# A new list of steps for linear attention and a highway layer on one core, with two weight rows to a partition and more work on GpSimd and ScalarE

## The chip, the cores and the metric

The kernel runs on one core of one Trainium2 chip. The metric is the device time of one execution in microseconds (us); the median of three runs before the change is 120.71 us (120.66 to 121.03).

A core has a matrix engine (TensorE, PE in the profile; PEld is its loading of the stationary operand), a vector engine (VectorE, DVE), an activation engine (ScalarE, ACT), a general engine (GpSimd, POOL) and a queue engine that only issues transfers (SyncE, SP). Transfers between the chip's main memory and the on-chip memory SBUF run on 16 DMA engines. PE writes its results to a second on-chip memory, PSUM, which POOL cannot reach.

## What is computed

The reference, cut to its core:

```python
# q, k, v: (8, 8, 576, 64) float32
q_s = softmax(q, over the 64 features);  k_s = softmax(k, over the 576 rows)
kv = np.einsum('bhsd,bhse->bhde', k_s, v)
x = np.einsum('bhsd,bhde->bhse', q_s, kv)            # as (4608, 512)
H = np.maximum(x @ w_h, 0.0)
T = 1.0 / (1.0 + np.exp(-(x @ w_t + b_t)))
out = T * H + (1.0 - T) * x                           # (4608, 512) float32
```

The kernel writes the gate as T = (1 + tanh(z/2))/2, so that out = x + (tanh(z/2) + 1) * d, with d = max(x @ (w_h - I)/2, -x/2).

## The kernel before

The program has no loops over tiles at run time. A text constant, ORDER (lines 16 to 62), names some 700 steps, and the last lines of the kernel (483 to 487) call one small function for each of them in that order. Each engine then carries out its own instructions strictly in the order in which they were issued to it; semaphores make an instruction wait for what it reads and for the buffers it overwrites. A step is written kind_number(_part)(:engine). The same list orders the DMA queue of SP (loads k, q, v, w and most stores st) and that of ACT (b, and stores marked :A).

The work: eight batches b of 576 rows, 36 tiles i of 128 output rows each. Batches go in pairs: tiles 0 to 3 are batch 0's, 4 to 7 batch 1's, and tile 8 takes the last 64 rows of both; nine tiles for each pair.

- Loads: `k_b_c`, `v_b_c`, `q_b_j`, `w_h_c`, `w_t_c` (two pieces of 512 KB each for both weight matrices, line 210). The number after the batch is the piece. Three buffers each for q, k, v.
- `ek` (line 252) exponentiates k on ACT, `eq` (lines 297 to 305) q on ACT; `vc` (line 258) casts v to 16 bits on ACT, DVE or POOL.
- `kv` (line 268): 72 small products a batch on PE. `kr` and `kn` (lines 280, 286): DVE divides by the sums and writes the block matrix `kvb`.
- `qt` (lines 316, 321): PE turns exp(q); `qc` (line 330) copies it to SBUF on ACT or DVE.
- `xu` (line 350): PE multiplies a tile of exp(q) by `kvb`. `rs` and `x` (lines 359, 365): DVE divides, giving the tile x (16 bit, six buffers `x16`).
- `xt` (line 372): four PE transposes of x into the PSUM tile `turned`; `xe` (line 379) copies them to SBUF on ACT or DVE.
- `bw` (lines 387, 389): puts the bias into the gate's PSUM bank, by a copy on ACT (:A) or by a PE product (no mark). `mt` (line 399) adds the four products with w_t, `mh` (line 407) makes the four with w_h. Two banks each, `ps_t` and `ps_g`.
- `th` (lines 421, 423): tanh on ACT. `dd` (line 427): DVE makes d (three buffers).
- `uu` is the blend: on DVE straight from PSUM (line 437), or, for tiles marked :P anywhere in the list, on POOL in two steps, `g` = tanh + 1 (line 434) and `u` = g * d (line 435). For such tiles `th` writes SBUF instead of PSUM. Three buffers each for g, u and the tanh.
- `oo` (line 455): out = u + x, on POOL except the last half tile. `st` (lines 463, 471, 475): stores; most tiles are stored two together.
- `fill_n` (line 167): n dummy PE products on a zero tile into the unused half of `turned`. They change no result.
- `whd` (line 225) subtracts the identity from w_h's blocks, `whc` and `wtc` (lines 231, 218 to 221) cast the weights; `bp`, `bc`, `bsplit` prepare the bias.

Tiles 0, 4 and 5 are worked in two halves (the second number of the step), so that they can start with half the heads. The last tile, 35, is blended and stored in two halves of 256 columns.

Of the kernel before, what the change touches and what calls it, by code (L numbers as in the profile page):

```python
# [16 lines left out]
b_0 b_32 k_0_2 ek_0_3 q_0_0 setuppool setupdve k_0_0 eq_0_0 v_0_0 v_0_3 v_0_2 ek_0_2 bsplit ek_0_1 fill_16 vc_0_0:A  # L17
fill_16 fill_16 qt_0_0 vc_0_2 q_0_4 v_0_1 bp vc_0_3:D fill_16 bc w_h_2 kv_0_1 fill_12 eq_0_1 qc_0_0 w_h_0 w_t_0 vc_0_1
qt_0_1 whd_2:P w_t_2 q_1_0 kr_0_1 ek_0_0 kn_0_1 kv_0_0 fill_2 k_1_2 bw_3 kr_0_0 kn_0_0 whd_1:P whd_0:P fill_9 xu_0_0
whd_3 eq_0_2 xu_1_0 v_1_2 qc_0_1:A whc_2:A rs_0_0 rs_1_0 qt_0_2 x_1_0 x_0_0 qc_0_2:A fill_12 xt_1_0 whc_0:A v_1_0  # L20
xe_1_0:D k_1_0 bw_1 xu_3_0 q_1_4 wtc_0 xu_0_1 rs_3_0 x_3_0 mh_1_0 wtc_2 xt_3_0 xe_3_0 xu_2_0 mt_1_0 rs_0_1 x_0_1
xt_0_0 eq_1_0 q_2_0 mt_3_0 th_1_0 rs_2_0 xe_0_0:D vc_1_3 ek_1_3 x_2_0 xt_0_1 th_3_0 qt_1_0 xe_0_1:D ek_1_2 dd_1
vc_1_0:A mh_0_0 xt_2_0 k_2_0 xe_2_0:D vc_1_2:D uu_1_0:P mh_0_1 bw_2 dd_0 qc_1_0:A mh_2_0 dd_2 vc_1_1 v_2_0 kv_1_1
mh_3_0 ek_1_0 bw_0 kr_1_1 kn_1_1 dd_3 ek_1_1 mt_2_0 xu_5_1 rs_5_1 xu_4_1 kv_1_0 rs_4_1 k_3_0 x_5_1 th_2_0 kr_1_0 bw_5
oo_1_0 xt_5_1 mt_0_1 kn_1_0 mt_0_0 xu_5_0 x_4_1 rs_5_0 eq_1_1 xu_4_0 qt_1_1 xe_5_1 mt_5_1 x_5_0 eq_1_2 qc_1_1 xt_5_0
xe_5_0:D mh_5_1 th_0_0 q_3_0 rs_4_0 eq_2_2 uu_0_0 xu_6_0 rs_6_0 xt_4_1 qt_1_2 mt_5_0 mh_5_0 v_3_0 bw_4 x_4_0 x_6_0
xe_4_1 th_5_0 xt_4_0 mh_4_1 uu_3_0:P qc_1_2:A xe_4_0 xu_8_0 mh_4_0 mt_4_1 xt_6_0 mt_4_0 eq_2_0 dd_5 oo_0_0 uu_2_0:P
rs_8_0 oo_3_0 vc_2_2 uu_5_0 qt_2_0 x_8_0 ek_2_2 xe_6_0:D ek_2_0 k_4_0 dd_4 xu_7_0 rs_7_0 bw_6 th_4_0 oo_5_0 xt_8_0
mh_6_0 mt_6_0 q_4_9 x_7_0 xe_8_0:D xt_7_0 vc_2_0:A qc_2_0 eq_2_1 uu_4_0 oo_4_0 dd_6 bw_7:A kv_2_0 th_6_0 bw_8:A ek_3_0
ek_3_2 oo_2_0 xe_7_0:D mh_8_0 kr_2_0 kn_2_0 dd_8 mt_7_0 xu_9_0 rs_9_0 x_9_0 qt_2_1 th_7_0 mt_8_0 q_4_0 qc_2_1 uu_6_0:P  # L30
xu_10_0 oo_6_0 xt_9_0 rs_10_0 x_10_0 th_8_0 xe_9_0 mh_7_0 uu_8_0 qt_2_2 dd_7 bw_9 xu_12_0 eq_3_1 eq_3_0 xt_10_0 mt_9_0
mh_9_0 rs_12_0 x_12_0 xe_10_0:D uu_7_0:P xu_11_0 qc_2_2 xt_12_0 rs_11_0 qt_3_0 x_11_0 bw_10:A vc_3_2 dd_9 xe_12_0:D
vc_3_0:A th_9_0 uu_9_0 mh_10_0 oo_8_0 kv_3_0 kr_3_0 dd_10 xt_11_0 mt_10_0 eq_3_2 qc_3_0:A bw_12:A oo_7_0 kn_3_0
mh_12_0 xu_14_0 ek_4_2 mt_12_0 xe_11_0:D v_4_0 v_5_0 qt_3_1 ek_4_0 rs_14_0 x_14_0 dd_12 xt_14_0 xe_14_0:D k_5_0
xu_13_0 th_10_0 bw_11:A rs_13_0 mh_11_0 mt_11_0 x_13_0 th_12_0 q_5_0 xt_13_0 qc_3_1:A oo_9_0 dd_11 uu_10_0:P xu_15_0
qt_3_2 uu_12_0 rs_15_0 mh_14_0 eq_4_0 xe_13_0:D eq_4_1 mh_13_0 x_15_0 oo_10_0 xu_16_0 xt_15_0 qc_3_2 dd_14 rs_16_0
qt_4_0 th_11_0 bw_14:A k_6_0 mt_14_0 x_16_0 qc_4_0 vc_4_2:A xe_15_0:D st_1_1 xu_17_0 st_1_0 rs_17_0 oo_12_0 x_17_0
qt_4_1 dd_13 bw_13:A mt_13_0 th_14_0 fill_0 vc_4_0 kv_4_0 uu_11_0:P eq_4_2 xt_16_0 qc_4_1:A mh_15_0 v_6_0 qt_4_2
vc_5_2 q_5_9 uu_14_0 xe_16_0:D st_3_1 oo_11_0 kr_4_0 th_13_0 oo_14_0 kn_4_0 bw_16:A bw_15:A xt_17_0 ek_5_0 xe_17_0:D
dd_15 mh_16_0 xu_18_0 qc_4_2:A rs_18_0 mt_16_0 ek_5_2 x_18_0 vc_5_0 th_16_0 uu_13_0:P mt_15_0 dd_16 uu_16_0 xt_18_0  # L40
# [25 lines left out]
def kernel(  # L66
# [49 lines left out]
    spare = turned[:, 1].rearrange("p c d -> p (c d)").bitcast(FP32)  # L116
# [48 lines left out]
    def fill(e, n):  # L165
        for _ in range(n):
            nc.tensor.matmul(spare, blank[:, 0:P], blank[:, 0:2 * P], start=True, stop=True,  # L167
                             skip_group_check=True)
# [38 lines left out]
    def load_w(e, w, c):  # L207
        src = dict(t=moe_w_t, h=moe_w_h)[w]
        T[f"w{w}{c}"] = op.tile([P, 2, DM], FP32, tag="o32", name=f"w32{w}_{c}")
        nc.sync.dma_start(T[f"w{w}{c}"], src.rearrange("(c p) n -> p c n", p=P)[:, c:c + 2])  # L210
# [12 lines left out]
    def wh_less_identity(e, c):  # L223
        block = T[f"wh{c // 2 * 2}"][:, c % 2, c * P:(c + 1) * P]
        (nc.gpsimd if e == "P" else nc.vector).tensor_sub(block, block, idf)
# [23 lines left out]
    def ek(e, b, c):  # L249
        n = 1 if b < 2 else 2  # L250
        t = once(f"ek{b}", lambda: ekp.tile([P, NJ, 4, D], FP16, tag="ek", name=f"ek_{b}"))
        nc.scalar.activation(t[:, :, c:c + n].rearrange("p j c d -> p c j d"),  # L252
                             T[f"k32{b}"][:, c:c + n].rearrange("p c (j d) -> p c j d", j=NJ), AF.Exp)
# [39 lines left out]
    def eq(e, b, g):  # L293
        t = once(f"qe{b}", lambda: qep.tile([P, NJ, 4, D], FP16, tag="qe", name=f"qe_{b}"))
        j0, j1 = GROUPS[g]
        if b not in WIDE:
            nc.scalar.activation(t[:, j0:j1].rearrange("p j c d -> p c j d"),  # L297
                                 T[f"q32{b}"].rearrange("p c (j d) -> p c j d", j=NJ)[:, :, j0:j1], AF.Exp)
        elif g < 2:
            src = flat_q(b)[:, 0:MAIN].rearrange("p (c hh j d) -> p c hh j d", c=4, hh=2, j=4)  # L300
            dst = t.rearrange("p j c d -> p (j c d)")[:, 0:MAIN]
            dst = dst.rearrange("p (j hh c d) -> p c hh j d", j=4, hh=2, c=4)
            nc.scalar.activation(dst[:, :, g], src[:, :, g], AF.Exp)
        else:
            nc.scalar.activation(t[:, 8], flat_q(b)[:, MAIN:].rearrange("p (c d) -> p c d", c=4), AF.Exp)
# [212 lines left out]
```

## Time and profile before

| | |
|---|---|
| median of three runs | 120.71 us |
| the profiled execution, its own time | 120.66 us |
| its span on the profile | 118.8 us |
| PE busy | 112.4 us (95%) |
| ACT busy | 95.1 us (80%) |
| DVE busy | 94.3 us (79%) |
| POOL busy | 83.0 us (70%) |
| moved by DMA | 40.08 MB, mean 337 GB/s |

The profile page gives each engine's busy time and the busy share of each of 40 equal slices of the span as a digit (9 means 90% or more). A group row reads: line, engine, operation, output<-inputs, shape, count | busy time in us, mean duration in ns | idle time of that engine just before. The timeline lists start and duration in us. A chain of waits is followed back from the last instruction to what released it. Matmuls overlap in the array and their ends are modelled, so the distance from one start to the next is PE's true pace.

Six groups by shape, from the same execution:

| group | count | busy us | mean ns |
|---|---|---|---|
| bias product on PE, 512 columns (L389) | 9 | 3.4 | 378 |
| bias copy on ACT (L387) | 26 | 15.3 | 594 |
| exp of k, 128x1152 (L252) | 12 | 13.5 | 1161 |
| exp of k, 128x576 (L252) | 8 | 5.3 | 678 |
| blend on POOL, g (L434) and u (L435) | 17 each | 10.5 and 19.6 | 618 and 1155 |
| blend on DVE, 512 columns (L437) | 18 | 12.3 | 685 |

### The profile page before, as it was taken

How to read it: one execution, taken by the hardware profiler on the slowest of the kernel's cores; microseconds unless marked ns; L12 is line 12 of the kernel's file. 1: busy time of each engine (PE TensorE's matmuls, PEld its weight loads, DVE VectorE, ACT ScalarE, POOL GpSimd, SP SyncE). 2: the span in 40 equal slices, each digit the busy share in tenths (PEclk: the TensorE clock that was granted, in tenths of full speed). 3: DMA queues.
4: the chain of work that ended last, by engine and by line, in shares of the span. 5: the costliest groups of instructions: out<-in, count | busy, mean ns of one | idle time of the engine just before them, and what ended most of it. 6: DMA issues, size and time to landing. Idle time of an engine off the chain costs nothing.

```text
span 118.8 us, 3618 instructions
## 1 busy us (share of the span) xinstructions
PE 112.4 (95%) x1440; PEld 70.7 (59%) x1440; DVE 94.3 (79%) x225; ACT 95.1 (80%) x144; POOL 83.0 (70%) x93
## 2 busy tenths in 40 slices
PE   5997999999999999999999999999999999999970
PEld 3785786645656665665565666565665655554560
DVE  5604277697999978999989999879896999879880
ACT  4265679969698999999999999949979987578420
POOL 5002240199095999939999997996798939999960
PEclk9999999999999999999999999999999999999999
DMA  2999999999999999999999999999999942995564
GB/s 91 352 376 384 386 376 379 394 370 387 392 386 392 389 389 385 336 376 386 391 375 361 404 387 394 348 357 385 394 389 336 338 110 88 395 287 204 200 253 168
DMA packets 22596, 40.08 MB, mean 337 GB/s; under 512 B 3250, under 2 KB 9650, under 8 KB 22580
## 3 DMA queue, kind: packets, MB, share of 16 engines
q1 hardware_dynamic: 22352, 39.46, 92.7%
q10 hardware_dynamic: 228, 0.40, 1.3%
q8 instruction: 11, 0.18, 0.6%
q14 instruction: 5, 0.04, 0.1%
HBM read 30.41 MB, written 9.44 MB: 335 GB/s over the span
## 4 chain that ended last, share of the span: by engine, by line
PE 56%; DMA 26%; SPq 5%; ACT 5%; DVE 2%; issue 2%; DVEq 0%
PE gps L407 19%; PE tps L399 19%; DMA v<-in_v_dram 12%; DMA w32t<-in_moe_w_t_dram 7%; DMA k<-in_k_dram 6%; PE turned L372 6%; PE xu L350 5%; PE qps L316 3%; PE kv L268 3%; SPq L183 3%; SPq L205 2%; DVE u L437 1%; PE qps L321 1%; ACT tps L387 1%; ACT v L258 1%
## 5 line engine op out<-in xcount | busy, mean ns | idle before, releaser
L455 POOL TENSOR_TENSOR o<-u,x 128x512 f32<-128x512 f16 (+1 forms) x36 | 40.5, 1142 | 6.1 <-DVE u L437 5.6
L399 PE MATMUL tps<-w16t,xT 128*128 128x512 f16 (+1 forms) x148 | 37.1, 373 | 0.0
L407 PE MATMUL gps<-w16h,xT 128*128 128x512 f16 x144 | 36.9, 380 | 0.0
L365 DVE TENSOR_TENSOR x<-xu,rs 128x512 f16<-128x512 f32 (+1 forms) x39 | 25.0, 647 | 2.4
L427 DVE SCALAR_TENSOR_TENSOR d<-x,gps 128x512 f16<-128x512 f16 x36 | 24.3, 676 | 0.2
L258 POOL CAST v<-v 128x1152 f16<-128x1152 f32 (+1 forms) x11 | 10.7, 970 | 18.9 <-DMA v<-in_v_dram 17.6
L252 ACT ACTIVATE ek<-k 128x1152 f16<-128x1152 f32 (+1 forms) x20 | 18.9, 968 | 3.1 <-DMA k<-in_k_dram 3.1
L435 POOL TENSOR_TENSOR u<-g,d 128x512 f16<-128x512 f16 x17 | 19.6, 1155 | 1.4
L399 PEld LDWEIGHTS <-xT 128*128 128x128 f16 x148 | 13.4, 98 | 10.3
L407 PEld LDWEIGHTS <-xT 128*128 128x128 f16 x144 | 12.6, 98 | 11.6 <-ACT xT L379 0.6
L387 ACT COPY tps<-ball 128x512 f32<-128x512 f32 x26 | 15.3, 594 | 1.6 <-DVE u L437 1.2
L167 PE MATMUL turned<-blank 128*128 128x256 f16 x111 | 14.8, 292 | 1.3 <-POOL blank L149 1.3
L372 PE MATMUL turned<-idh,x 128*128 128x128 f16 x144 | 14.4, 219 | 0.2 <-ACT xT L379 0.2
L350 PE MATMUL xu<-kvb,eq 128*128 128x130 f16 (+1 forms) x160 | 14.3, 224 | 0.0
L350 PEld LDWEIGHTS <-eq 128*128 128x128 f16 (+1 forms) x160 | 10.3, 100 | 6.8 <-DVE x L365 2.3
L437 DVE SCALAR_TENSOR_TENSOR u<-tps,d 128x512 f16<-128x512 f32 (+1 forms) x20 | 13.1, 658 | 1.5 <-ACT tps L423 1.2
L423 ACT ACTIVATE tps<-tps 128x512 f32<-128x512 f32 (+1 forms) x20 | 11.2, 561 | 3.5 <-PE tps L399 3.3
L167 PEld LDWEIGHTS <-blank 128*128 128x128 f16 x111 | 11.3, 105 | 3.6 <-POOL blank L149 1.3
L372 PEld LDWEIGHTS <-x 128*128 128x128 f16 x144 | 10.3, 98 | 4.8 <-DVE x L365 0.6
L297 ACT ACTIVATE qe<-q 128x1024 f16<-128x1024 f32 (+1 forms) x12 | 10.0, 842 | 3.9 <-DMA q<-in_q_dram 3.8
L379 DVE COPY xT<-turned 128x512 f16<-128x512 f16 (+1 forms) x28 | 11.3, 403 | 2.2 <-PE turned L372 1.9
L434 POOL TENSOR_SCALAR g<-th 128x512 f16<-128x512 f16 x17 | 10.5, 618 | 3.6 <-ACT th L421 3.6
(48 smaller groups left out, 120.9 us busy)
## 6 DMA issues: line engine op xcount, KB each, us to landing
k<-in_k_dram SPq DMA_DIRECT2D x6, 1152.0 KB, 14.7
v<-in_v_dram SPq DMA_DIRECT2D x6, 1152.0 KB, 11.6
out_dram<-o SPq DMA_DIRECT2D x22, 256.0 KB, 4.9
q<-in_q_dram SPq DMA_DIRECT2D x10, 512.0 KB, 9.1
out_dram<-o SPq DMA_DIRECT2D x6, 512.0 KB, 5.5
k<-in_k_dram SPq DMA_DIRECT2D x4, 576.0 KB, 6.9
q<-in_q_dram SPq DMA_DIRECT2D x2, 1152.0 KB, 14.0
q<-in_q_dram SPq DMA_DIRECT2D x2, 640.0 KB, 12.3
```

The source lines that it names most:

```text
L167: nc.tensor.matmul(spare, blank[:, 0:P], blank[:, 0:2 * P], start=True, stop=True, skip_group_check=True)
L252: nc.scalar.activation(t[:, :, c:c + n].rearrange("p j c d -> p c j d"), T[f"k32{b}"][:, c:c + n].rearrange("p c (j d) -> p c j d", j=NJ), ...
L350: nc.tensor.matmul(dst, turned_q(b, jp, n), kvb[b % NKV][:, hh, kk], start=True, stop=True, skip_group_check=True)
L365: nc.vector.tensor_mul(t[:, k0:k1], sums(i, k)[:, :, :, 0:64], T[f"rs{i}_{k}"][:, 0:k1 - k0].unsqueeze(3).to_broadcast([P, k1 - k0, 4, D]))
L372: nc.tensor.matmul(t[:, n], T[f"x{i}"][:, n * P:(n + 1) * P], idh, is_transpose=True, start=True, stop=True, skip_group_check=True)
L387: nc.scalar.copy(t[:, cs], ball[:, cs])
L399: nc.tensor.matmul(T[gate(i, k)][:, cs], T[f"xT{i}"][:, n], w16["t"][:, n, cs], start=False, stop=(n == parts[-1] and not first), skip_gro ...
L407: nc.tensor.matmul(t, T[f"xT{i}"][:, n], w16["h"][:, n], start=(first and n == parts[0]), stop=(n == parts[-1] and not (first and len(part ...
L427: nc.vector.scalar_tensor_tensor(t, T[f"x{i}"], -0.5, T[f"gps{i}"], op0=ALU.mult, op1=ALU.max)
L435: nc.gpsimd.tensor_mul(t, g, T[f"d{i}"])
L437: nc.vector.scalar_tensor_tensor(t[:, cs], T[gate(i, h)][:, cs], 1.0, T[f"d{i}"][:, cs], op0=ALU.add, op1=ALU.mult)
L455: eng.tensor_add(t[:, cs], T[f"u{i}"][:, cs], T[f"x{i}"][:, cs])
```

## The change

1. Each load of weights puts rows 2p and 2p+1 of a 256-row half on partition p, one piece of 4096 bytes, instead of rows p and p+128 as two pieces of 2048. The contraction index is therefore paired differently, and the identity block and the transposes of x follow: they take every second column.
2. Dummies multiply 512 columns instead of 256 and write the whole of `turned`.
3. From batch 2 on, exps of q are cut by pieces of the row block instead of by columns, and steps marked :F do in one instruction what two or three did: eq_2, ek_2, ek_3, ek_5, eq_5, ek_6 and eq_7 (whole, or all but the last 256 columns).
4. 20 tiles are blended on POOL instead of 17, and 30 biases are copied by ACT instead of 26. All four identity subtractions and the cast of one half of w_t are on POOL.
5. For the last half tile the blend stays in PSUM and the addition reads it there; halves have their own `u16` tile.
6. The whole list of steps is new. 14 stores are on ACT's queue instead of 2.

```diff
 ORDER = """
-b_0 b_32 k_0_2 ek_0_3 q_0_0 setuppool setupdve k_0_0 eq_0_0 v_0_0 v_0_3 v_0_2 ek_0_2 bsplit ek_0_1 fill_16 vc_0_0:A
-fill_16 fill_16 qt_0_0 vc_0_2 q_0_4 v_0_1 bp vc_0_3:D fill_16 bc w_h_2 kv_0_1 fill_12 eq_0_1 qc_0_0 w_h_0 w_t_0 vc_0_1
-qt_0_1 whd_2:P w_t_2 q_1_0 kr_0_1 ek_0_0 kn_0_1 kv_0_0 fill_2 k_1_2 bw_3 kr_0_0 kn_0_0 whd_1:P whd_0:P fill_9 xu_0_0
-whd_3 eq_0_2 xu_1_0 v_1_2 qc_0_1:A whc_2:A rs_0_0 rs_1_0 qt_0_2 x_1_0 x_0_0 qc_0_2:A fill_12 xt_1_0 whc_0:A v_1_0
...
+setuppool fill_8 fill_8 v_0_0 q_0_0 eq_0_0 fill_8 fill_8 v_0_1 setupdve k_0_0 vc_0_0 fill_8 v_0_3 vc_0_3 k_0_2 v_0_2
+b_0 q_0_4 b_32 w_h_0 bsplit bp ek_0_0 vc_0_1 ek_0_1 kv_0_0 ek_0_2 qt_0_0 ek_0_3 w_h_2 vc_0_2 kv_0_1 kr_0_1 whd_1:P
+qc_0_0:A w_t_2 whd_0:P kr_0_0 fill_6 bc kn_0_1 xu_0_1 kn_0_0 xu_1_0 xu_0_0 bw_1 w_t_0 eq_0_1 qt_0_1 rs_1_0 x_1_0
+whd_2:P whc_0:A k_1_2 xt_1_0 rs_0_1 whd_3:P qc_0_1 xe_1_0 whc_2:A v_1_2 bw_3 xu_3_0 rs_3_0 fill_6 rs_0_0 eq_0_2 x_3_0
+xt_3_0 xe_3_0 xu_2_0 x_0_1 wtc_2 ek_1_2 mh_1_0 qt_0_2 xt_0_1 x_0_0 qc_0_2:A xt_0_0 q_1_0 xe_0_0:D rs_2_0 mh_3_0
+wtc_0:P mt_1_0 k_1_0 mt_3_0 ek_1_3 dd_1 x_2_0 xe_0_1 xt_2_0 th_1_0 vc_1_3 uu_1_0:P mh_0_0 th_3_0 vc_1_2:D xe_2_0:D
+v_1_0 dd_3 kv_1_1 eq_1_0 uu_3_0:P ek_1_1 kr_1_1 kn_1_1 ek_1_0 vc_1_1 mh_0_1 dd_0 mh_2_0 dd_2 qt_1_0 qc_1_0 bw_2
+vc_1_0:A mt_2_0 xu_5_1 rs_5_1 oo_1_0 bw_0 x_5_1 xu_4_1 rs_4_1 kv_1_0 kr_1_0 kn_1_0 x_4_1 mt_0_1 xt_5_1 mt_0_0 th_2_0
...
+rs_7_0 bw_8:A x_7_0 vc_2_2:A mt_6_0 qt_2_1 th_6_0 mt_8_0 dd_6 kv_2_0 qc_2_1 oo_4_0 oo_5_0 kr_2_0 kn_2_0 xt_7_0
+xe_7_0:D th_8_0 qt_2_2 qc_2_2 mh_8_0 xu_9_0 rs_9_0 bw_7:A mh_7_0 x_9_0 dd_8 fill_1 bw_9:A uu_6_0:P xu_10_0 rs_10_0
...
+mt_32_0 x_35_0 th_33_0 uu_33_0 dd_32 xe_34_0 st_30_0 xt_35_0 bw_34:A mh_34_0 th_32_0 oo_33_0 mt_34_0 uu_32_0 st_33_0
+oo_32_0 st_32_0 xe_35_0 mh_35_0 bw_35_0 dd_34 mt_35_0 th_34_0 uu_34_0 oo_34_0 th_35_0 st_34_0 dd_35 uu_35_0 oo_35_0
+st_35_0 bw_35_1 mt_35_1 th_35_1 uu_35_1 oo_35_1:D st_35_1:A fill_1
 """
...
-    spare = turned[:, 1].rearrange("p c d -> p (c d)").bitcast(FP32)
+    spare = turned.rearrange("p a c d -> p (a c d)").bitcast(FP32)
...
-            nc.tensor.matmul(spare, blank[:, 0:P], blank[:, 0:2 * P], start=True, stop=True,
+            nc.tensor.matmul(spare, blank[:, 0:P], blank, start=True, stop=True,
                              skip_group_check=True)
...
-        nc.sync.dma_start(T[f"w{w}{c}"], src.rearrange("(c p) n -> p c n", p=P)[:, c:c + 2])
+        nc.sync.dma_start(T[f"w{w}{c}"], src.rearrange("(c p r) n -> c p r n", p=P, r=2)[c // 2])
...
-        block = T[f"wh{c // 2 * 2}"][:, c % 2, c * P:(c + 1) * P]
+        block = T[f"wh{c // 2 * 2}"][:, c % 2, c // 2 * 2 * P + c % 2:c // 2 * 2 * P + 2 * P:2]
...
     def ek(e, b, c):
-        n = 1 if b < 2 else 2
+        n = 1 if b < 2 else 4 if e == "F" else 2
...
+        if b in WIDE:
+            if g == 2:
+                nc.scalar.activation(t[:, 8], flat_q(b)[:, MAIN:].rearrange("p (c d) -> p c d", c=4), AF.Exp)
+                return
+            half = slice(0, 8) if e == "F" else slice(4 * g, 4 * g + 4)
+            src = flat_q(b)[:, 0:MAIN].rearrange("p (c t d) -> p c t d", c=4, t=8)[:, :, half]
+            nc.scalar.activation(t[:, half].rearrange("p t c d -> p c t d"), src, AF.Exp)
+            return
+        js, cs = slice(*GROUPS[g]), slice(0, 4)
+        if b >= 2:
+            js, cs = slice(0, NJ), slice(0, 4) if e == "F" else slice(2 * g, 2 * g + 2)
+        nc.scalar.activation(t[:, js, cs].rearrange("p j c d -> p c j d"),
+                             T[f"q32{b}"].rearrange("p c (j d) -> p c j d", j=NJ)[:, cs, js], AF.Exp)
...
-            nc.tensor.matmul(t[:, n], T[f"x{i}"][:, n * P:(n + 1) * P], idh, is_transpose=True,
+            n0 = n // 2 * 2 * P
+            nc.tensor.matmul(t[:, n], T[f"x{i}"][:, n0 + n % 2:n0 + 2 * P:2], idh, is_transpose=True,
                              start=True, stop=True, skip_group_check=True)
...
-        t = once(f"u{i}", lambda: dp.tile([P, DM], FP16, tag="u16", name=f"u16_{i}"))
+        if i == LAST and h == 1:
+            g = T[f"u{i}_1"] = T[gate(i, h)]
+            nc.vector.scalar_tensor_tensor(g[:, cs], g[:, cs], 1.0, T[f"d{i}"][:, cs], op0=ALU.add, op1=ALU.mult)
+            return
+        t = T[f"u{i}_{h}"] = dp.tile([P, DM], FP16, tag="u16", name=f"u16_{i}")
```

## The prediction

> **What bounds the kernel now.** I read the page's slices first, then the chain of waits in order of time, then each engine's timeline.
>
> ```profile
> PE   5997999999999999999999999999999999999970
> DVE  5604277697999978999989999879896999879880
> ACT  4265679969698999999999999949979987578420
> POOL 5002240199095999939999997996798939999960
> DMA  2999999999999999999999999999999942995564
> ...
> 18.99 1.04 PE L407 MATMUL gps<-w16h,xT 128*128 128x512 f16 x4
> ...
> 27.82 0.77 PE L268 MATMUL kv<-v,ek 64*64 64x65 f16 x36
> ...
> 31.00:45.00 14.00, 13.86 (x184) 8.43 (x183) 12.94 (x30) 12.79 (x20) 11.06 (x11) 1.00 1.05 390
> 45.00:60.00 15.00, 14.89 (x197) 9.10 (x197) 13.95 (x34) 14.97 (x22) 12.80 (x14) 1.00 1.07 375
> ...
> 79.89 0.22 PE tps L389
> 80.11 0.86 PE tps L399 x4
> ...
> 112.83 1.04 PE L399 MATMUL tps<-w16t,xT 128*128 128x256 f16 x8
> 114.83 0.66 DVE o L455
> ```
>
> The slices show PE full from the second slice on, at full clock, but its first 14 us are mostly dummies (L167). The timeline puts the first product with w_h at 18.99; from there PE has almost no gap until its last useful product starts at 112.83. The window rows (columns PE, PEld, DVE, ACT, POOL busy, clock, DMA share, GB/s) say that the others are nearly full as well: in 45 to 60 ACT has 14.97 of 15. The chain gives true paces: four 512-column products 0.86 us, one bias product 0.22; mean durations of matmul rows include a modelled end. So the time is three stretches: 27.82 us until kv_1_0 (second half of batch 1's K^T V), the PE list from there to its end at 113.71 (112.83 + 0.88, the eight half products at 0.11), and 5.1 us behind it.
>
> With these paces (products 0.216, transposes 0.056 a block, X products 0.235 a tile, kv 0.73 a batch) the list before has 83.7 us of useful PE work from kv_1_0 on. It took 113.71 - 27.82 = 85.9, so 2.2 us are small waits.
>
> **The change part by part.**
>
> *Start.* SP's queue keeps the amount ahead of each need: k_0_0 is again complete after 1664 KB (8.7 us before), the second 512 KB of w_h after 4480 KB (16.3). Walking the new list: 40 dummies of 512 columns from 1.32 on, at 0.216 each and about 1.5 us more while PE starts slowly (the 48 old ones of 256 took 6.8 us where 48 x 0.11 make 5.3), end at 11.5; bp and kv_0_0 to 12.4, qt_0_0 to 12.8, kv_0_1 (v_0_2 lands at 11.8, cast 0.67) to 13.3. kr and kn are four DVE steps of 0.17 to 0.59: to 14.9. xu_1, x_1, qc_0_1 (0.68), xu_3, x_3 follow one another on DVE to 18.55; six dummies end at 18.75; xt_3, xu_2, then mh_1 at 19.2 against 18.99, with 4.0 us of useful work done instead of 3.7. From there the needs (eq_1_0 after q lands at 23.0; v_1_0 at 26.1, cast to 26.7; on DVE dd_2, qc_1_0 until 27.2) bring kv_1_0 to 27.6, the same 12.2 us of useful work done as before. Worth **0.2 us**. Unknown inside it: the order differs at so many places that I allow from 1.0 earlier to 1.0 later.
>
> *4096-byte packets.* The weights' stretch (13.6 to 18.4) moves 377 GB/s, the stretch 31 to 45 with its 2304-byte packets 390: 2.1 MB gain at most 0.2 us. At the bottom nothing, since DVE sets mh_1. I take nothing.
>
> *What that layout asks of PE.* With rows 2p and 2p+1 on one partition, xt must load every second column of x (L372): 144 weight loads that step by two elements. No load of before does. From below it costs nothing; from above a load that no longer hides takes its row's whole 98 ns where a block now takes 56: 144 x 0.042 = 6.0 us. I take nothing, because a 64x64 load (L268 row, 106 ns) is no quicker than a 128x128 one: the duration is not set by the elements read. The Trainium skill (SBUF — State Buffer, Door 1) says that a read keeps full rate with two hits in each 16-byte line; this step gives four, so by it too nothing. No run shows such a load yet. The identity's subtraction steps alike: four on POOL (0.46) in place of three and one on DVE; from 0 to twice, 1.8 us, hidden behind the DVE chain above, else as much on mh_1.
>
> *Biases.* PE keeps bw_0, 1, 2, 3, 5 and tile 35's; bw_4, 6, 9, 22 go to ACT: 4 x 0.216 = **0.87 us off PE**, 4 x 0.59 = 2.4 on ACT. Behind each copy on ACT wait th and xe of the next tiles, and mt for the copy itself.
>
> *Joined exps.* The L252 rows give 678 ns for 576 elements and 1161 for 1152: 0.84 ns an element, 0.195 fixed. eq and ek from batch 2 on are 30 instructions before and 21 now: 9 x 0.195 = 1.75 us less on ACT. In return seven hold ACT for 1.9 to 2.13 instead of 1.16. ACT also loses five qc (3.8, to DVE), one wtc and one vc, and gains three xe: 2.9 us less in sum. Nothing on the path while it keeps up; a copy of bias or a th may come 1 us later behind each joined exp, 7 in all from above.
>
> *Blends.* Three more on GpSimd: 3 x (0.62 + 1.16) = 5.3 us, and with casts and weights 8.1 us more on POOL, 83.0 to 91. DVE gives up 3 x 0.69. Cover: before, POOL is busy for 78.1 of the 91.1 us from its first blend (24.1) to its end (115.2), so 13.0 idle. Its results free x16 (six tiles later), d16 and u16 (three later) and feed the stores. I take nothing, from above 5.8, all that rival 3 counts.
>
> *Stores.* 14 go out on ACT's queue instead of 2; each issue takes 0.23 to 0.54 there in the rows. The one at 93.89 ran beside a copy and cost ACT about 0.1: 14 x 0.1 = 1.4 us, in ACT's slack. It is also moved past SP's queue, where a load took up to 5.5 us to issue.
>
> *Dummies.* Wider ones only fill waits; fill_1 between mh_7 and xu_10 stands in the full stretch: **0.22 us on PE**. They now write all of `turned`, so fill_6 waits for xe_1 (done 17.4, xu_3 17.35).
>
> *Tail.* The last half blend is written to PSUM, and its addition reads it there: like the 128x256 x row, 0.41 instead of 0.66 beside POOL. In the new order th_35_1 ends 0.4 behind PE, uu_35_1 0.4, oo_35_1 0.4: 1.3 us against 115.49 - 113.71 = 1.8. **0.45 us**, from 0 (store already late) to 0.8.
>
> **Sum**: 118.8 - 0.2 - 0.87 + 0.22 - 0.45 = 117.5 of span, if the 2.2 us of small waits stay. Around the span lie 120.66 - 118.8 = 1.86, so **119.4 us**, 1.1% under the median of 120.71 (the profiled execution is 0.05 under it). The small waits may go (117.2) or double (121.6).
>
> **Rivals.**
>
> 1. *The gain is eaten by new small waits*: 1.3 us more, in a list that was full before. For it: ACT at 14.97 of 15; against: ACT and DVE have less to do. **120.7**.
>
> 2. *Stepped weight loads are slow*: slower than before. Place: xt on PE, in each of 36 tiles; price 0.042 a block, to 6.0 us, **125.4**. It decides from 0.009 us a block on (1.3 us in all). For it: PE has no slack to hide it. Against: the 64-wide loads above.
>
> 3. *GpSimd becomes the bound*: from its first blend (now 23.1) it has 78.1 + 5.3 = 83.4 us of work (the other 2.8 lie before it). To end by 113.7, as the forecast has it, it may idle 7.2 us where it idles 13.0 now. Its waits came from th and u of other engines, which the change does not remove; if half the difference of 5.8 stays, the last addition ends at 116.6, and with 118.8 - 115.5 = 3.3 behind it and 1.86 around it that is **121.8**; if all stays, 124.7. For it: between mh_12 and mh_16 POOL's steps add up to 15.7 us and PE's to 11.9 (before 11.6 and 12.5). Against: the six buffers of x16 cover 15 us of PE.
>
> 4. *ACT is held by its stores.* Six lie where SP's queue is still full; a store's issue there took 0.47 to 2.67 on SP (median 0.64). At 1 us each, 0.9 over what is counted above, ACT loses 5.4 us, and if half reaches PE the time is 119.4 + 2.7 = **122.1**. Against: at 0.73 one on ACT (0.52) ran beside one on SP (0.45). The Trainium skill (Perfetto Trace Analysis, Per-engine timelines) says that a queue locks the one descriptor generator for itself and waits for the lock; by it this rival would hold, and the overlapping rows at 0.73 show no such wait.
>
> **Chances.** Forecast 0.58, rival 1 0.14, rival 2 0.10, rival 3 0.11, rival 4 0.07. The measurement of this kernel can tell about 0.3% (0.36 us) from no change. The forecast's own range is 117.6 to 120.6, so a little of it is no change: faster 0.58 (the forecast 0.55, rival 1 0.03), same 0.10, slower 0.32. The likeliest case gives the time, 119.4. To hold 8 in 10 the range goes from 117.6 up past rivals 3 and 4 to 122.8, a third of the way to rival 3 at its worst, and leaves out rival 2.
>
> **What would show it.** Start: kv_1_0 (L268, third group) near 27.6. xt: the L372 groups of four still 0.22 apart in the chain; 0.39 means rival 2. Biases: five whole L389 products. Exps: rows of 128x2304 near 2.13 us. PE: no gaps over 0.3 behind 27.6, last product near 112.7; gaps released by ACT speak for rivals 1 and 4, by POOL, with POOL busy to the end, for rival 3. Wrong in another way: if DMA lands late, L252 or L258 waits of over 1 us behind 30.

## The result, and the profile after

The changed kernel takes 124.94 us (median of 4 runs, 124.00 to 125.03), the kernel before 120.87 beside it on the same chip: ratio 1.0316, 95% interval 1.0258 to 1.0373. It is slower, and lies 5.5 us above the forecast of 119.4. The profiled execution is the longest of the four: 125.03 us, span 123.2.

Two rows of the page's slices of the changed kernel, PE's busy tenths and the transfer rate:

```profile
PE   5999989999999999999998999999999798899920
...
GB/s 102 313 381 389 408 395 378 384 375 388 394 386 387 392 376 363 365 378 387 380 375 398 395 361 342 297 244 246 304 396 380 310 160 281 168 225 217 324 176 88
```

The transfer rate of the kernel before:

```profile
GB/s 91 352 376 384 386 376 379 394 370 387 392 386 392 389 389 385 336 376 386 391 375 361 404 387 394 348 357 385 394 389 336 338 110 88 395 287 204 200 253 168
```

Before, no slice between the second and the 32nd is under 336 GB/s. After, four slices in a row, from 77 to 89 us (a slice is 3.08 us), have 297, 244, 246 and 304, and between 95 and 108 us three of PE's slices fall to 7 and 8.

The timeline of the changed kernel, PE's lines and the last addition of VectorE (start, duration, engine, line, and in brackets the idle time just before and its releaser):

```profile
19.79 1.02 PE L410 MATMUL gps<-w16h,xT 128*128 128x512 f16 x4
...
28.32 0.48 PE L268 MATMUL kv<-v,ek 64*64 64x65 f16 x36
...
66.53 0.67 PE L268 MATMUL kv<-v,ek 64*64 64x65 f16 x59
68.02 0.29 PE L268 MATMUL kv<-v,ek 64*64 64x65 f16 x13 [0.82 <-issue]
...
93.62 0.41 PE L352 MATMUL xu<-kvb,eq 128*128 128x130 f16 x4 [0.23 <-DVE x L367]
96.77 0.77 PE L268 MATMUL kv<-v,ek 64*64 64x65 f16 x72 [0.79 <-DVE x L367]
102.23 1.02 PE L402 MATMUL tps<-w16t,xT 128*128 128x512 f16 x4 [0.21 <-ACT tps L390]
106.24 1.04 PE L410 MATMUL gps<-w16h,xT 128*128 128x512 f16 x4 [0.29 <-ACT xT L382]
...
116.96 0.60 PE L402 MATMUL tps<-w16t,xT 128*128 128x256 f16 x4
119.61 0.42 DVE L462 TENSOR_TENSOR o<-tps,x 128x256 f32<-128x256 f32 x1 [1.11 <-issue]
```

The three stretches of the prediction can be read off. kv_1_0 starts at 28.32 (forecast 27.6). PE ends at 116.96 + 4 x 0.11 = 117.40, so 89.08 us behind kv_1_0 (forecast 85.25, that is 83.05 of work and 2.2 of small waits). Behind that lie 123.2 - 117.40 = 5.8 us (forecast 4.65). The misses are 0.72, 3.83 and 1.15, together 5.7, the difference between the span and the 117.5 that was summed.

The windows of the changed kernel (columns as in the prediction):

```profile
31.00:45.00 14.00, 13.95 (x187) 8.06 (x185) 12.56 (x31) 13.18 (x17) 13.15 (x14) 1.00 1.05 389
45.00:60.00 15.00, 15.00 (x199) 9.49 (x196) 13.68 (x31) 14.04 (x19) 13.41 (x14) 1.00 1.07 374
74.00:92.00 18.00, 18.00 (x220) 10.69 (x218) 16.54 (x37) 15.56 (x21) 14.56 (x16) 1.00 0.94 303
```

Up to 60 us the kernel does what was forecast: PE is full, ACT is down from 14.97 of 15 to 14.04 in the second row, and POOL has taken work over. In the third row PE is still full, but only 303 GB/s are moved, after 389 and 374. What is missing there is felt later. The waits of the changed kernel name it (engine, line, what it waited for: us in total, times, longest):

```profile
POOL o L462 <- DMA out_dram<-o: 4.5, 2, 3.1
...
DVE x L367 <- POOL o L462: 1.3, 2, 0.8
...
SPq L198 <- DMA out_dram<-o: 4.6, 1, 4.6
```

GpSimd stands 4.5 us (3.1 before 91.7, 1.4 at the end) because an output buffer is not stored yet, VectorE then waits for GpSimd to release x, and TensorE for VectorE (93.62, 96.77). The last row is the odd one: on SP's queue a *load* (L198, the second half of q_7_0) waits 4.6 us for the landing of a *store*. The trace's operands say how: each transfer waits on a semaphore that an earlier transfer counted, and eight such semaphores go round over all transfers of the list, those of SP's queue and those of ACT's. This load waits on the one of st_3_0, which ACT issued only at 74.00; the load went out at 79.12. And the chain of waits of the changed kernel runs through two stores. The second lands only after 12.21 us: v_7 and k_7, which had been held, were issued ahead of it on the same queue (80.79 and 81.42), and k_7 itself landed at 94.22.

```profile
74.56 4.68 DMA out_dram<-o
...
84.61 12.21 DMA out_dram<-o
```

### The profile page after: what moved, and what is told of

Same layout as the page of the kernel before. It is cut to its first block, busy times and chain, and to the rows that moved or that the text cites. A ratio compares the mean times of both kernels' runs of the same rounds, so it can differ in the third digit from the quotient of the medians.

```text
span 123.2 us, 3484 instructions
## 1 busy us (share of the span) xinstructions
PE 113.4 (92%) x1379; PEld 64.1 (52%) x1379; DVE 93.0 (75%) x222; ACT 93.4 (76%) x135; POOL 91.5 (74%) x103
## 4 chain that ended last, share of the span: by engine, by line
PE 53%; DMA 17%; POOL 8%; DVE 6%; issue 4%; ACT 4%; SPq 3%; POOLq 1%; ACTq 0%; DVEq 0%
DMA out_dram<-o 17%; PE tps L402 13%; PE gps L410 13%; PE turned L167 10%; PE xu L352 4%; PE kv L268 4%; POOL u L442 4%; POOL o L462 3%; PE turned L375 3%; PE qps L323 3%; DVE kvb L286 2%; SPq L482 1%; SPq L183 1%; ACT tps L390 1%; DVE u L444 1%
## 5 line engine op out<-in xcount | busy, mean ns | idle before, releaser
L410 PE MATMUL gps<-w16h,xT 128*128 128x512 f16 x144 | 37.0, 379 | 0.3 <-ACT xT L382 0.3
L442 POOL TENSOR_TENSOR u<-g,d 128x512 f16<-128x512 f16 x20 | 23.2, 1158 | 2.1 <-DVE rs L361 0.5
L252 ACT ACTIVATE ek<-k 128x576 f16<-128x576 f32 (+2 forms) x16 | 18.1, 1159 | 5.1 <-DMA k<-in_k_dram 5.1
L390 ACT COPY tps<-ball 128x512 f32<-128x512 f32 x30 | 17.4, 589 | 4.1 <-DVE u L444 2.5
L410 PEld LDWEIGHTS <-xT 128*128 128x128 f16 x144 | 12.7, 98 | 12.2 <-ACT xT L382 1.0
L167 PE MATMUL turned<-blank 128*128 128x512 f16 x54 | 14.4, 422 | 1.3 <-POOL blank L149 1.3
L441 POOL TENSOR_SCALAR g<-th 128x512 f16<-128x512 f16 x20 | 12.4, 619 | 2.4 <-ACT th L424 2.3
L424 ACT ACTIVATE th<-tps 128x512 f16<-128x512 f32 x20 | 11.7, 593 | 2.0 <-PE tps L402 1.9
L444 DVE SCALAR_TENSOR_TENSOR u<-tps,d 128x512 f16<-128x512 f32 (+1 forms) x16 | 10.6, 671 | 3.4 <-ACT tps L426 2.8
L382 DVE COPY xT<-turned 128x512 f16<-128x512 f16 (+1 forms) x25 | 9.8, 397 | 3.8 <-PE turned L375 3.7
L306 ACT ACTIVATE qe<-q 128x1024 f16<-128x1024 f32 (+3 forms) x9 | 9.4, 1055 | 3.2 <-DMA q<-in_q_dram 3.2
L426 ACT ACTIVATE tps<-tps 128x512 f32<-128x512 f32 (+1 forms) x17 | 9.3, 554 | 2.2 <-PE tps L402 2.2
```

The costliest lines, as they stand in the source:

```text
L167: nc.tensor.matmul(spare, blank[:, 0:P], blank, start=True, stop=True, skip_group_check=True)
L390: nc.scalar.copy(t[:, cs], ball[:, cs])
L410: nc.tensor.matmul(t, T[f"xT{i}"][:, n], w16["h"][:, n], start=(first and n == parts[0]), stop=(n == parts[-1] and not (first and len(part ...
L441: nc.gpsimd.tensor_scalar(g, T[f"th{i}"], 1.0, 1.0, op0=ALU.add, op1=ALU.mult)
L442: nc.gpsimd.tensor_mul(t, g, T[f"d{i}"])
```

## The experiments

Each kernel was timed beside the kernel before. To see where a kernel gains, the table gives for each profiled execution the distance in us between the starts of the first w_h products (L410) of certain tiles; for tile 1 the start itself, and in the last row the distance to the end of the span (which is given to 0.1 us). Diffs of the list show only the steps that differ, without the rest of their lines.

| stretch | after | a_sp | a_two | a_early | a_late | a_bufs | a_sp_bufs | h2_f3 |
|---|---|---|---|---|---|---|---|---|
| mh_1 starts at | 19.79 | 20.12 | 20.44 | 20.31 | 19.65 | 19.93 | 19.96 | 19.28 |
| mh_1 to mh_16 | 43.48 | 43.47 | 43.49 | 43.61 | 43.56 | 43.49 | 43.58 | 43.95 |
| mh_16 to mh_17 (kv_5 in it) | 5.21 | 4.91 | 5.07 | 5.36 | 5.26 | 5.29 | 4.92 | 4.20 |
| mh_17 to mh_26 | 23.88 | 23.89 | 24.04 | 23.88 | 23.89 | 23.88 | 23.89 | 24.03 |
| mh_26 to mh_29 (kv_7 in it) | 5.35 | 4.09 | 4.20 | 4.09 | (6.73) | 5.61 | 4.09 | 4.09 |
| mh_29 to mh_30 | 8.53 | 7.19 | 8.53 | 8.54 | 7.19 | 8.54 | 7.19 | 7.19 |
| mh_30 to mh_35 | 9.21 | 9.02 | 9.21 | 9.20 | 9.02 | 9.20 | 9.03 | 9.02 |
| mh_35 to the end | 7.75 | 8.11 | 7.72 | 7.81 | 8.10 | 7.06 | 7.24 | 7.04 |

Kernels with the same start differ by 0.8 us in its first row, which no edit explains; within the other rows equal code gives equal time to some 0.2 us, so the stretches tell more than the medians.

### Four theories for the second half

**a_sp: the 13 late stores on SyncE.**

```diff
-st_3_1:A st_3_0:A st_7_0:A st_7_1:A st_8_0:A st_12_0:A
-st_12_1:A st_14_1:A st_23_0:A st_16_1:A st_25_0:A st_26_0:A st_21_0:A
+st_3_1 st_3_0 st_7_0 st_7_1 st_8_0 st_12_0
+st_12_1 st_14_1 st_23_0 st_16_1 st_25_0 st_26_0 st_21_0
```

> The changed kernel with 13 of its 14 stores on ScalarE's queue moved to SyncE's, at the same places of the list. Theory A (output path, held by the second queue: a load on SyncE waits for the landing of a store that ScalarE reaches late, 4.6 us at 74.5; the transfer engines fall to 244-304 GB/s between 74 and 92; output buffers stay full and GpSimd waits 4.5 us for them): most of the 3.8 us comes back, time 121.3 to 122.8, no slice under 330 GB/s between 70 and 90. Theory B (the list of steps puts the stores and loads in a bad order, whichever engine issues them): 124 to 126, the fall in GB/s stays. Theory C (GpSimd with 20 blends is the bound): 124.9 within 0.5.

122.70 us, ratio 1.0143 (1.0115 to 1.0171): 2.2 us come back, and no slice between 70 and 90 us is under 365 GB/s. The window row of this kernel, 74 to 92:

```profile
74.00:92.00 18.00, 18.00 (x220) 10.68 (x217) 16.53 (x37) 15.73 (x23) 17.46 (x19) 1.00 1.06 381
```

381 GB/s for 303, and GpSimd busy 17.46 us for 14.56. In the table two stretches close, by 1.26 and 1.34 us. Theory A holds; the list alone (B) and GpSimd's work (C) do not explain it.

**a_bufs: more output buffers.**

```diff
-    op = pool("op", 7)
+    op = pool("op", 9)
-            t = once(f"o{i}", lambda: op.tile([P, DM], FP32, tag="o1", bufs=3, name=f"o32_{i}"))
+            t = once(f"o{i}", lambda: op.tile([P, DM], FP32, tag="o1", bufs=5, name=f"o32_{i}"))
```

> The changed kernel with 9 two-tile output buffers for 7, and 5 one-tile ones for 3. Theory A in its second half (GpSimd stalls for want of a free output buffer, and VectorE and TensorE behind it): GpSimd's 4.5 us of waits for stores are gone, the two gaps of TensorE near 93 and 96 (0.23 and 0.79 us) with them, the tail falls by some 1 us: 122.3 to 123.6. If the buffers matter only because the loads are late too: 124.2 to 125. Theory C: 124.9 within 0.5.

124.07 us (123.66 to 124.78), in none of the expected ranges. The waits of GpSimd for a store are gone, and the last row of the table falls by 0.7. The gap of PE near 93 is gone too, but mh_26 to mh_29 takes 5.61, no less than after. What it waits for there stands in this kernel's timelines of PE and ACT:

```profile
97.26 0.78 PE L268 MATMUL kv<-v,ek 64*64 64x65 f16 x72 [1.22 <-ACT ek L252]
...
94.99 2.22 ACT L252 ACTIVATE ek<-k 128x1152 f16<-128x1152 f32 x2 [1.11 <-DMA k<-in_k_dram]
```

The exps of the last batch wait for k_7. So in this stretch the late loads decide, and the full buffers are a second wait beside them; for the tail the buffers decide.

**a_unjoin: the seven joined exps in two halves each.**

```diff
-eq_2_0:F
+eq_2_0 eq_2_1
-ek_2_0:F
+ek_2_0 ek_2_2
```

(and so for ek_3, ek_5, eq_5, ek_6 and eq_7)

> The changed kernel with the seven joined exponentials (2.12 us) cut into two of 1.06 to 1.09 us again, one behind the other at the same place. Theories A, B and C: no change, 124.9 within 0.5 (seven more fixed costs of some 0.02 us). Theory D (the long exponentials hold ScalarE's copies and TensorE waits for them): 123 or less, though two halves in a row hold ScalarE as long, so only what waits for the first half gains.

124.65 us (124.49 to 124.91), 0.3 less, within the spread of the changed kernel. Theory D falls.

**a_lift16: four blends back on VectorE.**

```diff
-uu_16_0:P uu_18_0:P uu_20_0:P uu_23_0:P
+uu_16_0 uu_18_0 uu_20_0 uu_23_0
```

> The changed kernel with the blends of tiles 16, 18, 20 and 23 on VectorE, so 16 on GpSimd in place of 20. GpSimd's work falls by 4 x 1.78 = 7.1 us, VectorE's grows by 4 x 0.67 = 2.7. Theory C: GpSimd's output additions come earlier, stores too, time 122.3 to 123.5. Theory A: GpSimd waits for its buffers instead, 124.4 to 125.2; VectorE at 75% has room, so no loss beyond 0.3.

131.75 us (131.70 to 132.14), 6.8 slower, which no theory expected. Its waits:

```profile
ACT tps L390 <- DVE u L444: 11.7, 10, 4.6
...
PE tps L402 <- ACT tps L390: 5.1, 4, 2.5
```

On VectorE a blend stands at its place of the list among the x and d steps, and holds the gate's PSUM bank until it is done; the next bias copy waits for the bank, and PE for the copy. For tiles blended on GpSimd the tanh goes to SBUF and the bank is free at once. So 20 blends on GpSimd are not the loss: this list needs them.

### Two losses in one queue

**a_two: two stores alone.**

```diff
-st_3_0:A st_7_0:A
+st_3_0 st_7_0
```

> The changed kernel with only two stores moved from ScalarE's queue to SyncE's: the halves of tiles 2 and 3 and of tiles 6 and 7 whose issue at 74.0 and 74.6 stands before the second half of the seventh sample's query load. Theory A1 (that load waits for the landing of a store that ScalarE reaches late): the load is issued by 75 in place of 79.1, and half or more of the 2.2 us that all 13 stores gave comes back, 122.6 to 123.8. Theory A2 (what costs is ScalarE's own issue time, 13 x 0.5 us): two of 13 give some 0.35 us, 124.4 to 124.8.

124.87 us (124.29 to 125.03): as a time, the expectation of A1 is missed, and A2's just so. In the trace A1 is right about the wait: the load is issued at 76.55 in place of 79.12 (by 75 was expected), and mh_26 to mh_29 falls to 4.20 by moving these two stores alone. In the profiled execution 0.65 of this is lost again by a later start (20.44).

**a_late and a_early: the last seven, or the first six, on SyncE.**

```diff
-st_12_1:A st_14_1:A st_23_0:A st_16_1:A st_25_0:A st_26_0:A st_21_0:A
+st_12_1 st_14_1 st_23_0 st_16_1 st_25_0 st_26_0 st_21_0
```

> The changed kernel with its last seven stores of ScalarE (issued from 97.9 to 110.4) on SyncE, and the first six left on ScalarE. Theory A2 (ScalarE's issue time, 3.8 us in the stretch 97.9 to 103.3, delays the bias copies and transposed copies that TensorE waits for there): the lag behind the all-SyncE kernel that opens between 97 and 107 (1.4 us of it) does not open, 123.3 to 123.8. Theory A1 (loads held by landings before 90): that lag stays, 124.5 to 125.

```diff
-st_3_1:A st_3_0:A st_7_0:A st_7_1:A st_8_0:A st_12_0:A
+st_3_1 st_3_0 st_7_0 st_7_1 st_8_0 st_12_0
```

> The changed kernel with its first six stores of ScalarE (issued from 62.8 to 89.9) on SyncE and the last seven left on ScalarE. If the two losses are separate: no lag behind the all-SyncE kernel up to the 114th product of gps (before 97), then the 1.35 us between the 114th and the 126th that the changed kernel has too; 123.7 to 124.5. If one hangs on the other: no lag anywhere, 122.7 to 123.2.

a_late took 124.31 us (123.53 to 125.42), between the two expected ranges, a_early 124.49 (124.00 to 124.94), at the upper end of the first. The table separates them: a_late has 7.19 and 9.02 in the stretches from mh_29, as with all stores on SyncE, while its load on SP's queue still waits 4.6 us for a store (its profiled execution was its longest, so the size 6.73 is not read); a_early has 4.09 up to mh_29 and keeps the loss behind it (8.54). There are two losses, of 1.26 and of 1.34 + 0.19 us, by two mechanisms. Moving one set alone, or the two stores of a_two, shows in the median by only 0.1 to 0.6, 0.8 to 1.1 less than in its stretches. The later starts (up to 0.65) and longer tails (up to 0.35) in the table are part of that; the rest stays open.

The second mechanism in the changed kernel's timeline of ACT (ACTq are the issues from its queue):

```profile
99.70 0.60 ACT L424 ACTIVATE th<-tps 128x512 f16<-128x512 f32 x1 [0.68 <-PE tps L402]
99.72 0.47 ACTq L482 DMA_DIRECT2D out_dram<-o  x1
100.29 0.60 ACTq L478 DMA_DIRECT2D out_dram<-o  x1
100.93 0.62 ACTq L482 DMA_DIRECT2D out_dram<-o  x1
101.59 0.59 ACT L390 COPY tps<-ball 128x512 f32<-128x512 f32 x1 [1.30 <-POOL g L441]
101.70 1.63 ACTq L478 DMA_DIRECT2D out_dram<-o  x1
102.12 0.59 ACT L424 ACTIVATE th<-tps 128x512 f16<-128x512 f32 x1
103.38 1.01 ACT L332 COPY eq<-qps 128x1024 f16<-128x1024 f16 x1 [0.67 <-issue]
```

The same steps with all stores on SyncE (a_sp):

```profile
98.47 0.60 ACT L424 ACTIVATE th<-tps 128x512 f16<-128x512 f32 x1 [0.71 <-PE tps L402]
99.09 0.59 ACT L390 COPY tps<-ball 128x512 f32<-128x512 f32 x1
```

In a_sp the bias copy follows the tanh by 0.02 us. After the change three issues stand between the two in ACT's queue; the first runs beside the tanh, the other two end at 101.55, and the copy starts at 101.59, 1.29 behind the end of the tanh. The row gives POOL's g as the releaser, but that had ended at 101.00, and by its operands the copy waits for nothing but ACT's own semaphore: what held it are the issues. A fourth issue, of 1.63 us, then holds the copy of exp(q) (L332) from the end of the tanh at 102.71 to 103.38, another 0.67. PE's gap at 102.23 follows the first hold, released by the bias copy. Counted from mh_29, PE is 0.38 us behind a_sp there, and 1.34 at mh_30 (106.24), behind both.

**b_act: the same 13 stores on ScalarE in the old list.** The diff is that of a_sp, reversed, on the list of before.

> The kernel before, its 13 stores that the change gives to ScalarE issued there, at their own places of the list, and nothing else. Theory A1: loads behind them on SyncE wait for landings that ScalarE's place decides, the transfer rate falls in the second half: 122 to 124. Theory A2: 13 x 0.5 us on an engine that is busy 80% of the time, some 0.3 to 1 us: 121.2 to 121.9. If the place of the stores in the new list is the whole cause, the second queue costs nothing here: 120.9 within 0.4.

123.57 us, ratio 1.0225 (1.0174 to 1.0277): 2.8 us slower, as A1 expected, and somewhat more than the 2.2 that the second queue costs the new list. Its waits show the same wait of a load (L199) for a store:

```profile
POOL o L456 <- DMA out_dram<-o: 3.8, 1, 3.8
...
SPq L199 <- DMA out_dram<-o: 4.1, 1, 4.1
```

In the kernel before, a load of q waits for a store 0.6 us at most, and GpSimd never does. So it is not a matter of the new list's places. A cluster of three issues (the third of 1.38 us) stands in this kernel as well, ahead of a gap of 0.49 on PE at 107.39, so the 2.8 is not A1's alone.

### Start, tail and biases

**a_sp_bufs: a_sp with the buffers of a_bufs.**

> The changed kernel with the 13 stores on SyncE's queue and with 9 and 5 output buffers. Theory A: the 1.7 us in which GpSimd, and the 1.4 us in which VectorE's last addition waits for a store go, and the tail behind the last product falls from 6.1 to 5.0 us: 121.3 to 122.0. If full buffers were only a consequence of the late loads, nothing is left to gain: 122.7 within 0.3.

122.00 us (121.73 to 122.45), 0.7 less than a_sp: the row mh_35 to the end goes from 8.11 to 7.24. No addition at the end waits for a store any more.

**h2_sp: the start of before.** The list of before up to kv_1_0, then the rest of the changed list in its order, all stores on SyncE; dummies 512 wide and half as many.

```diff
-setuppool fill_8 fill_8 v_0_0 q_0_0 eq_0_0 fill_8 fill_8 v_0_1 setupdve k_0_0 vc_0_0 fill_8 v_0_3 vc_0_3 k_0_2 v_0_2
+b_0 b_32 k_0_2 ek_0_3 q_0_0 setuppool setupdve k_0_0 eq_0_0 v_0_0 v_0_3 v_0_2 ek_0_2 bsplit ek_0_1 fill_8 vc_0_0:A
...
```

> The list of steps of before up to its product kv_1_0 (its dummies halved in number, since they are twice as wide), and behind it the changed list, with the stores on SyncE; all else as changed, the layout of the weights too. If the late start (kv_1_0 at 28.3 in place of 27.8) is the new list's, it starts by 27.9 and the end follows: 122.1 to 122.5, against 122.7 with the changed list throughout. If it is the layout or the dummies: 122.7 within 0.3.

122.01 us (121.84 to 122.25), 0.7 less than a_sp. kv_1_0 starts at 27.50, as expected. Since layout and wide dummies stayed, the late start is the new list's.

**h2_sp_bufs: both.**

> The start of before, the changed list behind it, all stores on SyncE, 9 and 5 output buffers. If the three costs (start 0.7, second queue 2.2, buffers 0.7) add up: 121.2 to 121.5; if the buffers' gain shrinks because the start moves: 122.0.

121.38 us, ratio 1.0036 (1.0011 to 1.0061). The three costs add up, and 0.5 us to the kernel before remain.

**b_bias: four biases on ScalarE, in the old list.**

```diff
-bw_4 bw_6 bw_9 bw_22
+bw_4:A bw_6:A bw_9:A bw_22:A
```

> The kernel before with the biases of tiles 4, 6, 9 and 22 copied by ScalarE in place of four products of 0.22 us, and nothing else. By the prediction's term: 119.9 to 120.2. Rival 1 (eaten by waits for ScalarE): 120.7 to 121.2, and waits of TensorE for a copy of the bias at these tiles.

121.84 us, ratio 1.0075 (1.0052 to 1.0098): 1.0 us slower, worse than rival 1 allowed. The gaps of PE in its timeline between 30 and 49:

```profile
33.46 0.27 PE L372 MATMUL turned<-idh,x 128*128 128x128 f16 x2 [0.29 <-ACT xT L379]
39.63 0.80 PE L268 MATMUL kv<-v,ek 64*64 64x65 f16 x72 [0.31 <-ACT v L258]
45.84 0.38 PE L372 MATMUL turned<-idh,x 128*128 128x128 f16 x4 [0.30 <-ACT xT L379]
```

PE hardly waits for the copies of the bias themselves, as was expected, but for other copies of ACT, which have more ahead of them now.

**b_parts: biases, layout and the last half tile in PSUM, in the old list.** The diff is that of b_bias with the lines of the change for `load_w`, `wh_less_identity`, `xt`, `uu` and `oo`.

> The kernel before with four parts of the change and its own list: weights two rows to a partition with the stepped transposes, the biases of tiles 4, 6, 9 and 22 on ScalarE, the last half tile multiplied in place. By the prediction's terms: 0.87 off TensorE and 0.45 off the tail, nothing for the layout: 119.3 to 119.8. If TensorE's saved products come back as waits for ScalarE (rival 1): 120.3 to 121.

121.51 us, ratio 1.0047 (1.0024 to 1.0069). It is no slower than b_bias, so layout and tail cost nothing; what they give, 0.3 us, is at the limit of what can be told.

**a_sp_pe: the four biases back on TensorE, in the new list (a_sp).**

```diff
-bw_4:A bw_6:A bw_9:A bw_22:A
+bw_4 bw_6 bw_9 bw_22
```

> The changed kernel with all stores on SyncE (122.7) and the biases of tiles 4, 6, 9 and 22 back on TensorE. If the prediction's term holds in the new list: 0.6 to 0.9 us slower, 123.3 to 123.6. If ScalarE's copies cost as much as they save: 122.7 within 0.3; if as in the old list: 121.5 to 122.

122.84 us (122.29 to 123.21) against 122.70 for a_sp, which the runs can't tell apart. The traces say more. Counted from mh_1, PE falls behind a_sp by some 0.2 us at each of the four products, by 0.78 in all at its last product: in the new list the copies do take off PE nearly what was summed. It does not reach the time of these runs: in the profiled executions a_sp_pe started 0.26 earlier, and its end is some 0.35 shorter, since in a_sp the last addition waits 1.41 us for a store.

### The gap at 67 us

Every kernel so far with the new list behind kv_1_0 has a pause inside the 72 products of kv_5_0 (the expectation below calls them kv_4_0, but kv_4_0 comes before mh_15), of 0.45 to 0.97 us, ended by "issue": nothing that the profile shows was waited for. None of the kernels with the old list has it there. The pause stands behind the 59th of these products with the new list, behind the 62nd in h2_sp and h2_sp_bufs, and behind the 56th in a_sp_pe, which has three more bias products ahead. Counted from the kernel's start, these are PE's products 862, 861 and 862: the pause keeps its place in the instruction stream, not at an operand.

**h2_f3: the dummies three times as many and a third as wide.** It is h2_sp_bufs with the same work in the dummies and, by the count of L167, 153 of them for 51: 100 more ahead of kv_5_0, each a weight load and a product, so 200 instructions and not the 164 of the expectation.

```diff
-            nc.tensor.matmul(spare, blank[:, 0:P], blank, start=True, stop=True,
+            nc.tensor.matmul(spare[:, 0:171], blank[:, 0:P], blank[:, 0:171], start=True, stop=True,
...
-fill_8
+fill_24
```

(and so for every other count of dummies)

> The kernel with the start of before, stores on SyncE and more buffers (121.4), its dummies three times as many and a third as wide (171 columns), so the same work of TensorE with some 164 more instructions ahead of kv_4_0. Fetch theory (the gap in kv_4_0 comes where a fetched block of instructions ends, 118 instructions into it): the end falls ahead of kv_4_0, the gap is gone there, 120.4 to 120.9. Data theory (an operand is late): the gap stays at the same product, 121.4 within 0.3.

120.49 us (120.06 to 120.72), ratio to the kernel before 0.9966 (0.9948 to 0.9984), and 0.9 less than h2_sp_bufs. The products of kv_5_0 in the timeline of h2_sp_bufs:

```profile
66.34 0.70 PE L268 MATMUL kv<-v,ek 64*64 64x65 f16 x62
67.93 0.28 PE L268 MATMUL kv<-v,ek 64*64 64x65 f16 x10 [0.89 <-issue]
```

and in that of h2_f3:

```profile
66.48 0.78 PE L268 MATMUL kv<-v,ek 64*64 64x65 f16 x72
```

The pause is gone, with the same data, the same list and the same stores; only the place of these products in the instruction stream moved, and the size of the dummies. That fits a fetch of instructions, and in the changed kernel's trace one of 16,384 bytes does run from 65.60 to 66.67. But it ends before the pause begins (67.2), and h2_f3 has one from 65.61 to 66.73 without a pause. That the pause hangs on the place in the stream is shown; that PE waits for a fetch is inferred.

**h2_f3_no: the same without the dummy between tiles 8 and 9 (three narrow ones here) and the one at the end.**

```diff
-fill_3 bw_9:A
+bw_9:A
```

> The same, without the one dummy between tiles 8 and 9 and the one at the end. By the prediction's 0.22 us for the former: 0.2 us less than its neighbour; if TensorE waits there anyway: the same within 0.1.

120.35 us, ratio 0.9952 (0.9931 to 0.9972). Of these kernels it is the fastest, 0.5 us under the kernel before. Its 0.14 under h2_f3 is within what cannot be told from no change. The traces settle the dummy between the tiles: from mh_7 to xu_10 it is 1.11 us with it and 1.10 without, so PE waits there anyway.

## Why the prediction was wrong

- **Start** ("worth 0.2 us", kv_1_0 at 27.6): wrong in sign, inside the 1.0 that was allowed. The dummies end at 11.95 for 11.5, mh_1 is at 19.79 for 19.2, kv_1_0 at 28.32. With the old start 0.7 us come back (h2_sp).
- **4096-byte packets and stepped weight loads** (nothing): right as far as it was tested (b_parts gives 0.3 us at most), and rival 2 is refuted by the rows that stand behind this list.
- **Biases** (0.87 off PE): nearly right for PE's work in the new list (0.78 in the trace of a_sp_pe, though the times do not show it), but no term that holds by itself: in the old list the same four copies cost 1.0, by what stands behind them on ACT.
- **Joined exps** (nothing): right. They take 2.12 to 2.13 us as worked out, and cutting them again gives nothing that can be told (a_unjoin). What joining saves is less than the 0.195 that was taken, since two halves one behind the other take 2.22.
- **Blends** (nothing; rival 3): right. POOL is busy 91.5 us, forecast 91, and taking blends away costs 6.8.
- **Stores** ("14 x 0.1 = 1.4 us, in ACT's slack"): this is the step that failed. The text saw the store "moved past SP's queue" and asked only what ACT's issue would cost. It missed that a load on SP's queue waits for the landing of a store on ACT's (1.26 us of PE), and that issues in a row hold the copies behind them, three by 1.29 and a fourth by 0.67 (together 1.34 + 0.19 of PE). a_sp gives 2.2 us back. Rival 4 named the second half at 122.1, with a chance of 0.07, but by way of a slow issue while SP's queue is full, at 1 us each. The issues took 0.34 to 0.62, but for one of 1.63, and those that held a copy came between 99 and 104, when SP issued nothing (95.5 to 108.7). The lock that the Trainium skill describes (Perfetto Trace Analysis, Per-engine timelines) did not show: SP's issue at 73.92 (0.60) and ACT's at 74.00 (0.49) overlap.
- **"If the 2.2 us of small waits stay"**: they did where the stores did not touch them, but for the pause of 0.82 in kv_5_0, which no view of the kernel before could show.
- **Dummies** (fill_1, 0.22 on PE): wrong by the traces, where it costs 0.01 (h2_f3_no); the medians (0.14) can't tell.
- **Tail** (0.45 less): wrong. The last additions wait 1.11 and 1.43 us for a buffer, so 5.8 us lie behind PE. With buffers enough it is 5.1 (h2_f3: 118.8 - 113.72), as before the change, not 4.65: the last addition ends 1.55 us behind PE instead of 1.78, but the span ends 3.5 us behind that, where it was 3.3.

The group row of the stepped weight loads in the changed kernel:

```profile
L375 PEld LDWEIGHTS <-x 128*128 128x128 f16 x144 | 9.9, 98 | 5.1 <-DVE x L367 1.6
```

and four of its transposes in the chain of waits:

```profile
19.49 0.22 PE turned L375 x4
```

A weight load that steps by two elements takes the 98 ns of the row of before, and four transposes still take 0.22; the Trainium skill (SBUF — State Buffer, Door 1) and the trace agree.

The sum of what was found: start 0.7, kv_5_0 0.8, loads behind stores 1.3, issues on ACT 1.5, tail 1.15, biases 0.1: 5.55 of 5.7 us. In h2_f3, whose stores are all on SyncE and which has no pause in kv_5_0, PE needs 113.72 - 28.10 = 85.6 us behind kv_1_0; the forecast was 85.25. So behind kv_1_0 the list itself does what was summed, and what was not in the sum there is the queues (2.8) and the pause.

## What to carry to other kernels

A second queue for stores is not free: its transfers stand in the order of the engine that issues them, and where transfers share semaphores, a load on the first queue may wait for a store on the second. Look up on which semaphore each load waits before moving a store, and do not put several issues between a result that is awaited and the copy behind it. An engine that is busy 75% to 80% can still be the one that everything behind a moved step waits for, so a move that saves 0.2 us on the full engine should be tried in its list before it is counted.

## What the runs showed of the hardware

- A pause of 0.45 to 0.97 us inside a run of 64x64 products, which depended on where the run lies in the instruction stream (always behind product 861 or 862; 0.89 in h2_sp_bufs, none in h2_f3), worth 0.9 us of 121.4.
- An issue of a store took 0.34 to 0.62 us of ACT's queue (one 1.63). The first ran beside the instruction ahead of it, but a second and third in a row held what stands behind (1.29), and so did the one of 1.63 (0.67).
- Weight loads with a step of two elements: 98 ns, as without.
